# Converting the last stage's weights further ahead of the blocks that use them (three chained layers, one Trainium2 core)

## The chip, the cores and the metric

The program runs on one core of one Trainium2 chip. The metric is the device time of one execution in microseconds (us). The kernel before takes 586.35 us (median of three runs, 586.0 to 589.92).

## The reference

Three layers stand one behind the other; the first two are told in short, since the change touches only the third.

```python
def _moe2_ref(x, w_in, w_out):            # x: 1536 x 512, d_ff = 2048
    h = x @ w_in
    r = np.maximum(h, 0.0)
    g = r * r
    return (g @ w_out).astype(np.float32)

def reference(**kwargs):
    attn_out = _attn_ref(**attn_kwargs)   # windowed attention with block summaries
    x = attn_out.transpose(0, 2, 1, 3).reshape(B * S, H * D)
    x = _moe_ref(x=x, **moe_kwargs)       # each token to one of 8 experts, 192 tokens each
    return _moe2_ref(x=x, **moe2_kwargs)
```

All data are float32.

## The kernel before, in words

`attention` computes the first layer, `moe` the second and the third. The last stage of `moe` is the third layer. Its input x stands in the on-chip tiles `yhi` and `ylo`: a value rounded to the narrower type fp32r, and what the rounding leaves. The weights `w_in` and `w_out` are split in the same way into `whi` and `wlo`, and each product is made of three matmuls (hi x hi, lo x hi, hi x lo).

**Blocks.** The stage has 48 blocks: 3 groups `j` of 512 tokens, and in each 16 slices `f` of 128 columns of d_ff (L1071). `hmm(i)` (L1074) makes one 128 x 512 slice of h with 12 matmuls (L1083) into a PSUM tile `pg`, of which there are four. ScalarE (ACT) takes the relu (L1086) into `xa` or `xb`, VectorE (DVE) squares it (L1087), ACT rounds it (L1092) and DVE takes the rest (L1093); both go to a tile `xt` or `ht`. `omm(i)` (L1096) multiplies that with `w_out`: 12 matmuls (L1110) into the accumulators `ph` and `px`. The loop at L1130 gives TensorE (PE) first `hmm(i)`, then `omm(i - 2)` (`LAG = 2`), so a block's own second half follows two blocks later.

**Conversion.** The weights come in as 32 pieces of 128 x 512 values, each a pair of 32-bit words per value (L613: four quarters of d_ff, in each four pieces of `w_in`, then four of `w_out`). `conv_stream` (L635) makes a piece usable in four steps, and each step puts one instruction on DVE: L647, L651 and L657 assemble the float32 value `f` from the raw words, then ACT rounds it into the hi tile (L650) and DVE subtracts for the lo tile (L654). The rounding of a piece stands in the second step of the piece behind it and its subtraction in the third, so piece n is done with the third step of piece n + 1; `ndone` (L655) counts the finished pieces, `nstep` the steps. The raw words lie in a tile `raw` with two buffers; when L657 has read a piece, SyncE's queue issues the load of the piece two further on (L662, L627). A piece lands in the hi and lo tiles of its quarter, named `w2a`, `w2b` or `w`.

**When steps are placed.** Some steps are recorded while the experts of the second layer run (L1019): 60 steps are recorded ahead of block 0, so 14 pieces are done there. In the last stage there are three sources: one step inside each block, behind the square (L1088); `SF` steps behind each block (L1139, `SF` at L417); and a `while` loop ahead of a block (L1134), which puts as many steps as are missing until `need` pieces are done. `need` (L1133) is what block i itself uses: for `hmm(i)` all four `w_in` pieces of quarter i // 4, for `omm(i - 2)` the `w_out` pieces up to its own. There are 4 steps to a block, so the steps recorded ahead of block i are 60 + 4i until the `while` loop has to help; it has to at block 12, whose quarter ends with piece 27.

The order of the instructions on each engine is that in which the program records them (`manual_schedule`, L1155): DVE takes squares, rests and conversion steps in one row, and an instruction that waits holds those behind it.

Of the kernel before, what the change touches and what calls it, by code (L numbers as in the profile page):

```python
# [413 lines left out]

BIG = 2.0 ** 120
CS = 2.0 ** 100
SF = 3  # L417


class Clock:  # L420
# [175 lines left out]
def moe(tc, nc, R0, x_dram, m_dram, L9, w1, w2, win, wout, out, identf, identb, dbg=None):  # L596
# [74 lines left out]
    def conv_step(n=1):  # L671
        for _ in range(n):
            if w2b or nstep[0] < 32:
                nstep[0] += 1
                next(CST, None)
# [396 lines left out]
    LAG = 2  # L1072

    def hmm(i):  # L1074
        j, f = seq[i]
        ps = p_g.tile([128, 512], F32, name="pg")
        whi, wlo = W[0, f // 4]
        fs = slice(128 * (f % 4), 128 * (f % 4) + 128)
        js = slice(512 * j, 512 * j + 512)
        n = 0  # L1080
        for k in range(4):
            for a, b in ((whi, yhi), (wlo, yhi), (whi, ylo)):
                nc.tensor.matmul(ps, a[:, k, fs], b[:, k, js], start=(n == 0), stop=(n == 11))  # L1083
                n += 1
        r = f1.tile([128, 512], F32, name="xa" if i % 2 else "xb")
        nc.scalar.activation(r, ps, AF.Relu)  # L1086
        nc.vector.tensor_tensor(r, r, r, op=OP.mult)  # L1087
        conv_step()  # L1088
        nm = ("xt", "xt", "ht")[i % 3]
        gg = f1.tile([128, 2, 512], F32R, name=nm, bufs=2 if nm == "xt" else 1)  # L1090
        ghi, glo = gg[:, 0, :], gg[:, 1, :]
        nc.scalar.activation(ghi, r, AF.Copy)  # L1092
        nc.vector.tensor_tensor(glo, r, ghi.bitcast(F32), op=OP.subtract)  # L1093
        GG[i] = ghi, glo
# [34 lines left out]

    for i in range(len(seq) + LAG):  # L1130
        if i < len(seq):
            last = i - LAG
            need = max(8 * (i // 4) + 4 if i < 16 else 0, 8 * (last // 4) + 5 + last % 4 if 0 <= last else 0)  # L1133
            while ndone[0] < min(len(todo), need):  # L1134
                conv_step()
            hmm(i)
        if i >= LAG:
            omm(i - LAG)
        conv_step(SF)  # L1139
    ctx.close()  # L1140


@with_exitstack
def kernel(ctx: ExitStack, tc: tile.TileContext, q, k, v, wg, w1, w2, win, wout, out):
    nc = tc.nc
    const = ctx.enter_context(tc.tile_pool(name="const", bufs=1))
    dram = ctx.enter_context(tc.tile_pool(name="dram", bufs=1, space=bass.MemoryType.DRAM))
    identf = const.tile([128, 128], F32, name="identf")
    make_identity(nc, identf)
    identb = const.tile([128, 128], BF, name="identb")  # L1150
    nc.vector.tensor_copy(identb, identf)
    L9 = const.tile([128, NBLK, E + 1], F32, name="L9")
    x_dram = dram.tile([N, DM], F32, name="x_dram")
    m_dram = [dram.tile([N], F32, name=f"m_dram{i}") for i in range(E)]
    ctx.enter_context(tc.manual_schedule())  # L1155
    route = Route(tc, nc, L9, identf)
    with ExitStack() as actx:
        attention(actx, tc, nc, q, k, v, wg, x_dram, L9, identf, identb, route)
    moe(tc, nc, route, x_dram, m_dram, L9, w1, w2, win, wout, out, identf, identb)
# [29 lines left out]
```

## Time and profile before

| | |
|---|---|
| median of the runs (three) | 586.35 us (586.0 to 589.92) |
| the profiled execution's own time | 587.83 us |
| span of its instructions | 585.6 us |
| TensorE (PE) matmul busy | 569.4 us, 97% of the span |
| VectorE (DVE) busy | 342.8 us, 59% |
| ScalarE (ACT) busy | 197.4 us, 34% |
| granted TensorE clock, mean | 0.996 of full speed |

The span runs from the first to the last instruction that the profiler recorded; the rest of the execution's time lies around it. Busy times are sums of the instructions of an engine. Matmuls overlap one another, so PE's distance from start to start is what counts, not the length of one row. A releaser behind an arrow is the instruction that ended a wait.

### The profile page before, as it was taken

What the parts mean: (1) busy time and instruction counts of PE and PEld (TensorE: products, weight loads), DVE (VectorE), ACT (ScalarE), POOL (GpSimd) and SP (SyncE); (2) the same over time, 40 slices, a digit from 0 to 9 for tenths busy, and PEclk for the clock granted to TensorE, in tenths of its full rate; (3) what the DMA queues carried; (4) which work ended last, traced back from release to release, by engine and by line L of the source; (5) the groups of instructions that cost most, each with busy time, mean ns of one, the idle gap of its engine ahead of it and who ended that gap; (6) DMA issues with size and microseconds to landing.
All of it is one profiled execution on the core that took longest, in us unless ns stands there. A gap on an engine that the chain in (4) does not pass through costs nothing.

```text
span 585.6 us, 10523 instructions
## 1 busy us (share of the span) xinstructions
PE 569.4 (97%) x4131; PEld 475.4 (81%) x4131; DVE 342.8 (59%) x773; ACT 197.4 (34%) x421; POOL 79.7 (14%) x136
## 2 busy tenths in 40 slices
PE   7999998999999999999999999799999999999996
PEld 4778873698998989899998888588888888888884
DVE  5885688877878779766566766663322222222222
ACT  4887861331422314123223333232222122222221
POOL 6564400210201132020000000000300000300002
PEclk9999999999999999999999999999999999999999
DMA  8997224645644455789742323320100000100001
GB/s 223 240 200 144 92 75 140 225 136 203 226 160 160 156 199 179 253 265 403 234 157 72 113 105 108 109 72 2 72 2 0 1 0 1 72 1 0 1 0 72
DMA packets 55392, 71.33 MB, mean 122 GB/s; under 512 B 21296, under 2 KB 32560, under 8 KB 55344
## 3 DMA queue, kind: packets, MB, share of 16 engines
q1 hardware_dynamic: 53360, 64.38, 35.5%
q0 software_dynamic: 1984, 6.29, 3.1%
q8 instruction: 32, 0.52, 0.4%
q14 instruction: 16, 0.13, 0.1%
HBM read 64.37 MB, written 6.29 MB: 121 GB/s over the span
## 4 chain that ended last, share of the span: by engine, by line
PE 76%; issue 13%; DVE 4%; DMA 2%; POOL 1%; ACT 1%; SPq 1%; POOLq 0%; DVEq 0%; ACTq 0%
PE pg L1083 15%; PE ph L976 15%; PE ph L993 15%; PE ph L1110 11%; PE px L1110 4%; PE O L284 2%; PE cnt L582 2%; DMA rawq<-in_q_dram 2%; PE T L270 2%; DVE G L570 2%; PE S L250 2%; POOL out_dram L1123 1%; PE ms L534 1%; PE T L193 1%; PE T L321 1%
## 5 line engine op out<-in xcount | busy, mean ns | idle before, releaser
L976 PE MATMUL ph<-xt,w 128*128 128x192 f32 x512 | 90.6, 330 | 0.0
L570 DVE TENSOR_SCALAR G<-mrow,m 128x1536 bf16<-128x1536 f32 (+4 forms) x108 | 84.7, 839 | 8.1 <-ACT mrow L537 4.8
L993 PE MATMUL ph<-ht,w 128*128 128x192 f32 x512 | 89.4, 329 | 0.0
L993 PEld LDWEIGHTS ph<-ht,w 128*128 128x128 f32 x512 | 82.9, 190 | 2.9 <-issue 2.5
L976 PEld LDWEIGHTS ph<-xt,w 128*128 128x128 f32 x512 | 82.5, 190 | 2.8 <-issue 2.1
L1083 PE MATMUL pg<-yhi,w 128*128 128x512 f32 x192 | 60.0, 392 | 3.2 <-DVE w L654 2.2
L1087 DVE TENSOR_TENSOR xa<-xa 128x512 f32<-128x512 f32 x24 | 16.6, 693 | 65.9 <-ACT xa L1086 65.9
L1087 DVE TENSOR_TENSOR xb<-xb 128x512 f32<-128x512 f32 x24 | 16.6, 693 | 62.9 <-ACT xb L1086 62.9
L1123 POOL DMA_INDIRECT out_dram<-f,sci x6 | 5.9, 978 | 306.7 <-DVE f L1121 306.1
L1083 PEld LDWEIGHTS pg<-yhi,w 128*128 128x128 f32 x192 | 36.0, 188 | 12.3 <-DVE w L654 3.1
L1086 ACT ACTIVATE xa<-pg 128x512 f32<-128x512 f32 x24 | 14.4, 599 | 78.2 <-PE pg L1083 78.2
L1086 ACT ACTIVATE xb<-pg 128x512 f32<-128x512 f32 x24 | 14.4, 599 | 73.7 <-PE pg L1083 73.7
L981 ACT ACTIVATE ht<-ph 128x384 f32<-128x384 f32 x32 | 15.7, 491 | 65.2 <-PE ph L976 61.5
L1083 PE MATMUL pg<-ylo,w 128*128 128x512 f32 x96 | 37.4, 389 | 0.0
L1110 PE MATMUL ph<-w,xt 128*128 128x512 f32 x144 | 36.8, 402 | 0.0
L1110 PEld LDWEIGHTS ph<-w,xt 128*128 128x128 f32 x144 | 28.0, 194 | 6.0
L1083 PE MATMUL pg<-yhi,w2a 128*128 128x512 f32 x96 | 29.7, 391 | 0.0
L1083 PE MATMUL pg<-yhi,w2b 128*128 128x512 f32 x96 | 29.6, 389 | 0.0
L999 ACT ACTIVATE yhi<-ph 128x384 fp32r<-128x384 f32 x16 | 7.9, 492 | 58.4 <-PE ph L993 58.4
L263 ACT ACTIVATE P<-S,nm 128x120 f32<-128x120 f32 x96 | 26.7, 374 | 2.4 <-DVE nm L259 2.4
L905 POOL DMA_INDIRECT xa<-x_dram,sci x8 | 10.8, 1355 | 87.2 <-DVE sci L893 65.3
L1083 PEld LDWEIGHTS pg<-yhi,w2b 128*128 128x128 f32 x96 | 18.0, 188 | 3.8
(245 smaller groups left out, 984.4 us busy)
## 6 DMA issues: line engine op xcount, KB each, us to landing
w<-in_moe_w_dram SPq DMA_DIRECT2D x64, 512.0 KB, 6.1
raw<-in_moe_w_in_dram SPq DMA_DIRECT2D x14, 512.0 KB, 4.0
raw<-in_moe_w_out_dram SPq DMA_DIRECT2D x14, 512.0 KB, 3.2
vw<-in_v_dram SPq DMA_DIRECT2D x16, 240.0 KB, 6.7
rawk<-in_k_dram SPq DMA_DIRECT2D x8, 384.0 KB, 6.8
rawq<-in_q_dram SPq DMA_DIRECT2D x8, 384.0 KB, 6.6
x_dram<-x SPq DMA_DIRECT2D x10, 256.0 KB, 2.3
w<-in_moe_w_in_dram SPq DMA_DIRECT2D x2, 512.0 KB
```

Of the source, the lines that this page charges most:

```text
L250: nc.tensor.matmul(ss[hh][64 * par:64 * par + 64, i, :], QT[b, hp][r, 128 * c + 64 * par:128 * c + 64 * par + 64], KW_[b, hp][r, 2 * c + p ...
L263: nc.scalar.activation(P[u][:, hh, i], SS[u][hh][:, i], AF.Exp, bias=NM[u][:, hh, i:i + 1])
L270: nc.tensor.transpose(ps[0:KW, i, :], P[u][:, hh, i, :], identf)
L570: self.nc.vector.tensor_scalar(t[:, used:used + w], self.mrow[:, 128 * j0:128 * j1], self.m[:, c:c + 1], CS, op0=OP.is_le, op1=OP.mult)
L976: nc.tensor.matmul(ps[:, j, 0:CAP], w[:, k, 128 * (f % 4):128 * (f % 4) + 128], d["xt"][:, k, :], start=(k == 0), stop=(k == 3), skip_grou ...
L981: nc.scalar.activation(d["ht"][:, f0:f0 + 2, :], ps[:, :, 0:CAP], AF.Relu)
L993: nc.tensor.matmul(ps[:, j, 0:CAP], w[:, f % 4, 128 * dd:128 * dd + 128], d["ht"][:, f, :], start=(f == 0), stop=(f == 7), skip_group_chec ...
L1083: nc.tensor.matmul(ps, a[:, k, fs], b[:, k, js], start=(n == 0), stop=(n == 11))
L1086: nc.scalar.activation(r, ps, AF.Relu)
L1087: nc.vector.tensor_tensor(r, r, r, op=OP.mult)
L1110: nc.tensor.matmul(PO[j][t], a[:, 128 * t:128 * t + 128], b[:, f % 4, :], start=(f == 0 and n == 0), stop=(f == 15 and n == 2))
L1123: sc = nc.gpsimd.indirect_dma_start(out=out, out_offset=bass.IndirectOffsetOnAxis(ap=sci[:, 4 * j + t:4 * j + t + 1], axis=0), in_=o, in_o ...
```

## The change

Two edits in the last stage. `SF` becomes 4: five conversion steps to a block, one inside and four behind. And the `while` loop ahead of block i asks for what block i + 2 uses: the `w_in` quarter of `hmm(i + 2)` and the `w_out` piece of `omm(i)`.

```diff
-SF = 3
+SF = 4
...
     for i in range(len(seq) + LAG):
         if i < len(seq):
-            last = i - LAG
-            need = max(8 * (i // 4) + 4 if i < 16 else 0, 8 * (last // 4) + 5 + last % 4 if 0 <= last else 0)
+            need = max(8 * ((i + LAG) // 4) + 4 if i + LAG < 16 else 0, 8 * (i // 4) + 5 + i % 4)
             while ndone[0] < min(len(todo), need):
                 conv_step()
             hmm(i)
```

The number of instructions on each engine stays as it was; PE's row and SyncE's row keep their order, DVE's and ACT's rows are interleaved in another way.

First place: DVE before, from block 9's square (`xa`, first row) to block 10's (`xb`) and on to its rest. `w_4648` is the lo tile of `w_out`'s third quarter, `w_4806` that of `w_in`'s fourth.

```order
L1087 TENSOR_TENSOR xa<-xa 128x512
L651 SCALAR_TENSOR_TENSOR f<-raw,f 128x512
L1093 TENSOR_TENSOR xt<-xa,xt 128x512
L654 TENSOR_TENSOR w_4648<-f,w_4647 128x512
L657 SCALAR_TENSOR_TENSOR f<-raw,f 128x512
L647 TENSOR_SCALAR f<-raw 128x512
L1087 TENSOR_TENSOR xb<-xb 128x512
L651 SCALAR_TENSOR_TENSOR f<-raw,f 128x512
L1093 TENSOR_TENSOR xt<-xb,xt 128x512
```

Each block has its square, one step, its rest and three steps; piece 24, the first of the fourth quarter, is not yet finished here.

The same place on DVE now, from block 9's square to block 10's. `w_4760` is the lo tile of `w_in`'s fourth quarter.

```order
L1087 TENSOR_TENSOR xa<-xa 128x512
L654 TENSOR_TENSOR w_4760<-f,w_4759 128x512
L1093 TENSOR_TENSOR xt<-xa,xt 128x512
L657 SCALAR_TENSOR_TENSOR f<-raw,f 128x512
L647 TENSOR_SCALAR f<-raw 128x512
L651 SCALAR_TENSOR_TENSOR f<-raw,f 128x512
L654 TENSOR_TENSOR w_4760<-f,w_4759 128x512
L657 SCALAR_TENSOR_TENSOR f<-raw,f 128x512
L647 TENSOR_SCALAR f<-raw 128x512
L651 SCALAR_TENSOR_TENSOR f<-raw,f 128x512
L654 TENSOR_TENSOR w_4760<-f,w_4759 128x512
L1087 TENSOR_TENSOR xb<-xb 128x512
```

Block 9 has one step and four, and the `while` loop ahead of block 10 adds the four rows from the second L657 on; the last L654 finishes piece 27.

Second place: DVE before, from block 11's rest (`ht`) to block 12's square (`xb`), with `w_4806` as above.

```order
L1093 TENSOR_TENSOR ht<-xa,ht 128x512
L654 TENSOR_TENSOR w_4806<-f,w_4805 128x512
L657 SCALAR_TENSOR_TENSOR f<-raw,f 128x512
L647 TENSOR_SCALAR f<-raw 128x512
L651 SCALAR_TENSOR_TENSOR f<-raw,f 128x512
L654 TENSOR_TENSOR w_4806<-f,w_4805 128x512
L657 SCALAR_TENSOR_TENSOR f<-raw,f 128x512
L647 TENSOR_SCALAR f<-raw 128x512
L651 SCALAR_TENSOR_TENSOR f<-raw,f 128x512
L654 TENSOR_TENSOR w_4806<-f,w_4805 128x512
L1087 TENSOR_TENSOR xb<-xb 128x512
```

Three steps are block 11's own and six are the `while` loop's; the last L654 finishes piece 27, which block 12's own first half reads.

The same place now: block 11's rest to block 12's square. `w_4871` is the lo tile of `w_out`'s fourth quarter.

```order
L1093 TENSOR_TENSOR ht<-xa,ht 128x512
L651 SCALAR_TENSOR_TENSOR f<-raw,f 128x512
L654 TENSOR_TENSOR w_4871<-f,w_4870 128x512
L657 SCALAR_TENSOR_TENSOR f<-raw,f 128x512
L647 TENSOR_SCALAR f<-raw 128x512
L1087 TENSOR_TENSOR xb<-xb 128x512
```

Only block 11's own four steps stand here, and they belong to `w_out`.

## Rows read from the trace of the kernel before

**Rows 1.** The page: the span, and PE's busy tenths in 40 equal slices.

```profile
span 585.6 us, 10523 instructions
...
PE   7999998999999999999999999799999999999996
```

**Rows 2.** The chain that ended last around 370: start us, us, what.

```profile
366.78 2.73 PE pg L1083 x12
373.55 3.21 DMA raw<-in_moe_w_out_dram
379.39 3.64 PE ph L1110 x9
```

**Rows 3.** Waits from 301 to 586: total us, times, longest us.

```profile
PEld pg L1083 <- DVE w L654: 3.1, 3, 2.0
PE pg L1083 <- DVE w L654: 2.2, 2, 1.7
...
PE pg L1083 <- ACT w L650: 1.1, 2, 0.5
```

**Rows 4.** Timeline of PE, blocks 11 to 13: start us, us, instruction, [idle before].

```profile
366.62 0.61 PE L1083 MATMUL pg<-yhi,w 128*128 128x512 f32 x2
...
369.34 2.20 PE L1110 MATMUL ph<-w,xt 128*128 128x512 f32 x9
...
372.06 0.61 PE L1083 MATMUL pg<-yhi,w 128*128 128x512 f32 x2
...
378.66 0.50 PE L1083 MATMUL pg<-yhi,w 128*128 128x512 f32 x1 [1.66 <-DVE w L654]
...
379.23 3.80 PE L1110 MATMUL ph<-w,xt 128*128 128x512 f32 x9
...
383.56 0.61 PE L1083 MATMUL pg<-yhi,w 128*128 128x512 f32 x2
```

**Rows 5.** Windows: stretch, length, busy us of PE, PEld, DVE, ACT, POOL; clock, DMA.

```profile
312.00:372.06 60.06, 60.06 (x268) 49.72 (x266) 41.02 (x70) 21.81 (x37) 0.00 (x0) 1.00 0.32 104
...
377.50:383.56 6.06, 4.90 (x15) 3.88 (x15) 4.41 (x8) 1.83 (x3) 0.00 (x0) 0.72 0.29 107
...
383.56:495.00 111.44, 111.44 (x493) 92.33 (x492) 34.90 (x53) 27.52 (x45) 4.82 (x8) 1.00 0.04 16
```

**Rows 6.** Timeline of DVE in block 12, out of the `while` loop's steps.

```profile
372.83 0.69 DVE L657 SCALAR_TENSOR_TENSOR f<-raw,f 128x512 int32<-128x512 int32 x1
...
376.85 0.43 DVE L647 TENSOR_SCALAR f<-raw 128x512 int32<-128x512 int32 x1 [1.06 <-DMA raw<-in_moe_w_out_dram]
...
377.92 0.68 DVE L654 TENSOR_TENSOR w<-f,w 128x512 fp32r<-128x512 f32 x1
```

**Rows 7.** Timeline of DVE, block 9 from its square to block 10's square.

```profile
359.35 0.69 DVE L1087 TENSOR_TENSOR xa<-xa 128x512 f32<-128x512 f32 x1 [1.81 <-ACT xa L1086]
359.96 0.68 DVE L651 SCALAR_TENSOR_TENSOR f<-raw,f 128x512 int32<-128x512 int32 x1
...
361.35 0.69 DVE L654 TENSOR_TENSOR w<-f,w 128x512 fp32r<-128x512 f32 x1
361.95 0.69 DVE L657 SCALAR_TENSOR_TENSOR f<-raw,f 128x512 int32<-128x512 int32 x1
362.56 0.42 DVE L647 TENSOR_SCALAR f<-raw 128x512 int32<-128x512 int32 x1
...
364.79 0.69 DVE L1087 TENSOR_TENSOR xb<-xb 128x512 f32<-128x512 f32 x1 [1.81 <-ACT xb L1086]
```

**Rows 8.** The source line L627 from 310 to 400: its loads, issue to landing.

```profile
DMA to landing us min/median/max: 3.1/3.7/4.5
```

**Rows 9.** Timeline of DVE and PE at the stage's start, blocks 0 and 1.

```profile
317.16 0.69 DVE L1093 TENSOR_TENSOR xt<-xb,xt 128x512 fp32r<-128x512 f32 x1
...
318.37 0.69 DVE L657 SCALAR_TENSOR_TENSOR f<-raw,f 128x512 int32<-128x512 int32 x1
...
320.38 2.20 PE L1110 MATMUL ph<-w2a,xt 128*128 128x512 f32 x9
...
323.17 0.43 DVE L647 TENSOR_SCALAR f<-raw 128x512 int32<-128x512 int32 x1 [0.58 <-DMA raw<-in_moe_w_in_dram]
```

## The prediction

> **What bounds the kernel now.** I read the page first. PE's row is made of nines but for the first, seventh and last slice and a 7 in the 26th of 40, which runs from 366.0 to 380.6 us (585.6 / 40 = 14.64 each) [rows 1]. The chain that ended last comes next: around that place it consists of PE's matmuls, leaves PE for a load of raw weights at 373.55, and is back on PE at 379.39 [rows 2]. Then the waits of the last stage: PE and its weight loads wait there for nothing but the converted weights, released by L654 on DVE and L650 on ACT [rows 3]. PE's timeline gives the price [rows 4]. A block is 5.44 us from start to start (366.62 to 372.06): 2.72 for the first half (L1083), 2.72 for the second (L1110). Block 12, which starts at 372.06, takes until 383.56, which is 11.50. So one block is 6.06 late. No other stretch of the stage holds such a loss: PE is busy for all of the 60.06 us ahead of it and all of the 111.44 behind it, at a clock of 1.00 [rows 5].
>
> The 6.06 has two parts. The first half of block 12 lasts 7.17 (372.06 to 379.23) where 2.72 is normal: 4.45 of waiting. The second half lasts 4.33 (379.23 to 383.56) where 2.72 is normal, though nothing is waited for: 1.61 that the lower clock costs. The granted clock from 377.50 to 383.56 is 0.72 on the mean, a mixture of the two levels 1.2 and 2.4 GHz, after an engine that had been stopped four times [rows 4, 5].
>
> Why it waits: 60 + 4 x 12 = 108 steps stand ahead of block 12, and piece 27 is done with step 4 x 28 + 2 = 114. The six missing steps are placed between block 11 and block 12, and PE reads the pieces as they come. One of the six also waits 1.06 for its raw words, because the load could be issued only after L657 at 372.83 [rows 6].
>
> **The change part by part.** Nothing is added or removed on any engine; the 68 steps left for the stage (128 less 60) come sooner.
>
> *SF from 3 to 4.* Steps ahead of block i become 60 + 5i. That is 110 ahead of block 10 and 115 ahead of block 11, so step 114 falls among block 10's own: this edit alone would finish piece 27 before block 12. Its cost lies on DVE. In a block of before, DVE works from the square at 359.35 to the end of the third late step at 362.98, 3.63 us, and is then idle for 1.81 until the next square at 364.79 [rows 7]. Steps follow one another by 0.57 on the mean (0.61, 0.60 and 0.61 for the three long ones, 0.46 for L647). A fifth step makes it 4.20 of 5.44 and leaves 1.24 idle. On the path this is 0: PE hides it, as long as DVE's waits stay under 1.24 per block.
>
> What DVE may wait for is the raw words. A load is issued when L657 of the piece two earlier is through, and L647 needs it five steps later. With five steps to a block that is one block from start to start, 5.44, or 4.75 from the end of L657. From the end of one L657 (318.37 + 0.69 = 319.06) to the L647 that waited for its load (323.17) it took 4.11 [rows 9]; landing alone takes 3.1 to 4.5 [rows 8]. I take 4.11, the row that holds issue and landing together: 0.64 is left, so no wait in regular blocks. With 4.5 and the same 0.1 of issue it would still fit, by 0.15.
>
> The stage's start is the tight place, since the first three first-halves follow each other by 2.72. Block 0's rest (L1093) ends at 317.85 and is needed by the second half at 320.38 [rows 9]: 2.53 to spare, and the added step stands behind it. For block k the need moves by 5.44 and DVE's row by 4.20 plus waits, so the room is 2.53 + 1.24k minus the waits so far. One wait of 0.58 is in the rows [rows 9]; with the fifth step I expect some 0.5 to 1 for each of the first four blocks, less than the room gained. Cost 0.
>
> *The look-ahead.* Ahead of every block up to 9 the 60 + 5i steps already satisfy it. At block 10 it asks for 28 pieces, step 114, with 110 done: four steps are placed ahead of block 10's square. PE's times up to there are those of before, so block 9's rows serve [rows 7]. L657 of piece 26 stands where L654 was, 361.35 to 362.04, and frees the buffer for piece 28. Three steps follow, then the burst: L657 at 363.6, and L647 of piece 28, ready at 364.2. Its load lands 4.11 after 362.04, at 366.15 (by the longest landing 366.65), a new wait of 1.9 to 2.4. Behind it in DVE's row stand two steps and block 10's square. Piece 27 is done 1.76 after the wait, at 367.9 to 368.4. PE reads it from 372.06 on: 3.7 to 4.2 to spare. The square of block 10 starts at 367.3 to 367.8, up to 3.0 later than the 364.79 of before, and the rest ends by 369.9; PE needs it at 374.78 (372.06 + 2.72). 4.9 to spare. What else hangs on the square is a PSUM tile that PE wants four blocks on. So the burst is hidden, and cost and gain of the look-ahead by itself are 0; without the fifth step it would have had to place 14 steps there (114 - 100), about 8 us and more loads to wait for.
>
> *What is late next.* The `w_out` pieces: second half 12 needs piece 28 and comes behind block 14's first half; 120 steps stand ahead of block 12 and step 118 is enough. All 32 pieces are done in block 12 or 13, about three blocks sooner. Nothing is late.
>
> **The sum.** Against the profiled execution: 587.83 - 6.06 = 581.77; the 2.23 around its span stays. The runs have a median of 586.35, 1.48 lower. The wait of 4.45 follows from the order of instructions and the length of the steps, so it is in every run. Of the 1.61 I can't say that: the profiled execution is longer than the median by nearly this much, so the runs may have had less of it. From the median the ends are 586.35 - 4.45 = 581.90 and 586.35 - 6.06 = 580.29. I take half of the clock's share, 4.45 + 0.81 = 5.26, as nothing in the rows puts it nearer to one end: 581.1.
>
> **Rivals.**
> *The whole clock share is in every run.* The clock falls because the engine stands still, so what removes the standstill gives back 1.61 too: 580.3. For it: 0.72 here, and 1.00 ahead and behind [rows 5]. Against it: the distance of the profiled execution from the median. By the Trainium skill, page "TensorE: Matmul & The Clock Gate", section "Part 1: The HAM clock gate", the slow clock is the state of an idle engine and steady work releases it; by that rule the time is this rival's, and the trace agrees in the one execution that it shows. The same section says that the point of the change moves from run to run, which speaks for less than the whole in some.
>
> *A part of the wait stays.* If loads under the quicker pace take so long that piece 27 is later than 372.06, block 12 waits again. That needs some 4 us more than I worked out, and the DMA engines are busy for 0.32 of their time there [rows 5]. If half of the stall stays, 583.3.
>
> *DVE becomes the bound, and it is slower.* The place is DVE's row in blocks 0 to 12. If each block waits for raw words by w, the lag grows by w - 1.24 a block. Over 13 blocks, less the room of 2.53 at the start, PE would lose 13(w - 1.24) - 2.53; this passes 6.06 from w = 1.90 on. With w = 2.3, about the burst's wait in every block, it loses 11.3 and the time is 586.35 - 5.26 + 11.3 = 592.4. Against it: in the blocks of before DVE waits for the square and not for loads [rows 7], and 4.75 is more than the longest landing [rows 8].
>
> *The change doesn't do what it says.* Excluded by the order: the last L654 of the awaited tile stands ahead of block 10's square.
>
> **How the numbers follow.** Forecast (581.1, its own range 580.3 to 581.9) 0.54; whole clock share (580.3) 0.33; a part stays (583.3) 0.10; slower 0.03. A run can tell about 1% here, which is 5.86 us, time 580.49. Three quarters of the whole-share case and a third of the forecast's lie beyond it, 0.25 + 0.18 = 0.43. Slower by over 1% has only its own case, 0.03; the rest, 0.54, is within 1%. The range takes the two ends of the sum, 1.1 below for the scatter of the runs (their lowest is 0.35 under the median), and above the case in which half of the stall stays: 579.2 to 584.0.
>
> **What would show it.** Right: in the profile after, all blocks from 3 on are 5.44 apart, PE's waits for L654 and L650 in the last stage are gone, the slice with the 7 is a 9, the clock is 1.00 there, and the conversions end about three blocks sooner. DVE shows a wait of about 2 at an L647 ahead of block 10's square, and PE none behind it. Wrong: a wait of PE for `xt` or `ht` (L1093) in blocks 0 to 12, for W pieces at block 12, or a stretch below clock 1.00 without a wait.

## The result, and the profile after

The changed kernel takes 581.17 us (median of four runs, 580.91 to 581.62); the kernel before, with one more run, 586.6 (586.0 to 589.92). The ratio is 0.9897, with a 95% interval of 0.9859 to 0.9934: 5.4 us less, and the interval reaches from 3.9 to 8.3. The forecast was 581.1. The profiled execution took 581.22.

The page of the changed kernel, its span and PE's busy tenths, which answer to [rows 1]:

```profile
span 579.0 us, 10522 instructions
...
PE   6999998999999999999999999999999999999995
```

The 7 in the 26th slice has become a 9. The span is 6.6 shorter than before. TensorE's timeline shows where that is; it answers to [rows 4] and holds the starts of blocks 11, 12 and 13:

```profile
366.06 0.62 PE L1083 MATMUL pg<-yhi,w 128*128 128x512 f32 x2
...
371.50 0.62 PE L1083 MATMUL pg<-yhi,w 128*128 128x512 f32 x2
...
374.21 2.20 PE L1110 MATMUL ph<-w,xt 128*128 128x512 f32 x9
...
376.94 0.62 PE L1083 MATMUL pg<-yhi,w 128*128 128x512 f32 x2
```

Block 12 takes 5.44 (371.50 to 376.94) like its neighbours, where it took 11.50. That is 6.06. The other 0.56 lies ahead of the stage: block 0 starts at 311.47 where it started at 312.03, though nothing was changed ahead of it, and block 11 at 366.06 where it started at 366.62. Such shifts from execution to execution are why the blocks are compared here and not the spans. The windows answer to [rows 5]; the columns are the same:

```profile
312.00:372.06 60.06, 60.06 (x266) 49.68 (x266) 49.26 (x84) 23.45 (x40) 0.00 (x0) 1.00 0.40 128
372.06:383.56 11.50, 11.50 (x53) 9.51 (x52) 8.26 (x14) 4.26 (x8) 0.00 (x0) 1.00 0.11 42
383.56:495.00 111.44, 111.44 (x493) 92.30 (x492) 30.30 (x45) 27.35 (x45) 7.08 (x13) 1.00 0.03 12
```

PE is busy throughout and the clock is 1.00. DVE's work has moved forward: 49.26 ahead of 372.06 where it was 41.02, and less behind. In the waits from 295 on, the rows of PE for L654 and L650 [rows 3] are gone. What is left is 0.3 of PE's weight loads for L1093, which the kernel before had too, and DVE's waits for raw words:

```profile
DVE f L647 <- DMA raw<-in_moe_w_out_dram: 2.4, 4, 1.2
...
PEld ph L1110 <- DVE ht L1093: 0.3, 1, 0.3
```

Two of these four waits, 1.0 in all, lie ahead of the stage. In the stage DVE waits 1.4 for raw words, where it waited 1.8 before. (`w_in` and `w_out` come as 64-bit values: on the page, the load of one 128 x 512 piece is 512 KB. So not all data are float32, and this is why the pieces have to be converted.)

The burst that the look-ahead places ahead of block 10's square, in DVE's timeline, out of its rows:

```profile
360.78 0.68 DVE L657 SCALAR_TENSOR_TENSOR f<-raw,f 128x512 int32<-128x512 int32 x1
...
363.05 0.69 DVE L657 SCALAR_TENSOR_TENSOR f<-raw,f 128x512 int32<-128x512 int32 x1
364.90 0.43 DVE L647 TENSOR_SCALAR f<-raw 128x512 int32<-128x512 int32 x1 [1.16 <-DMA raw<-in_moe_w_out_dram]
365.36 0.69 DVE L651 SCALAR_TENSOR_TENSOR f<-raw,f 128x512 int32<-128x512 int32 x1
365.97 0.68 DVE L654 TENSOR_TENSOR w<-f,w 128x512 fp32r<-128x512 f32 x1
366.57 0.69 DVE L1087 TENSOR_TENSOR xb<-xb 128x512 f32<-128x512 f32 x1
```

The reader is to see a real wait of 1.16 that costs nothing: L654 finishes piece 27 at 366.65, and block 12 starts at 371.50. The last conversion ends at 379.79, in block 13; in the kernel before it ended at 400.74, in block 16.

### The profile page after: what moved, and what is told of

It is laid out like the page before. It is cut to its first block, busy times and chain, and to the rows that moved or that the text cites. A ratio compares the mean times of both kernels' runs of the same rounds, so it can differ in the third digit from the quotient of the medians.

```text
span 579.0 us, 10522 instructions
## 1 busy us (share of the span) xinstructions
PE 565.8 (98%) x4131; PEld 473.7 (82%) x4131; DVE 343.7 (59%) x773; ACT 197.0 (34%) x421; POOL 78.6 (14%) x136
## 3 DMA queue, kind: packets, MB, share of 16 engines
q0 software_dynamic: 1984, 6.29, 3.2%
HBM read 64.37 MB, written 6.29 MB: 122 GB/s over the span
## 4 chain that ended last, share of the span: by engine, by line
PE 78%; issue 14%; DVE 3%; DMA 2%; POOL 1%; SPq 1%; ACT 1%; POOLq 0%; DVEq 0%; ACTq 0%
PE pg L1083 16%; PE ph L976 15%; PE ph L993 15%; PE ph L1110 11%; PE px L1110 4%; PE O L284 2%; PE cnt L582 2%; PE T L270 2%; DMA rawq<-in_q_dram 2%; DVE G L570 2%; PE S L250 2%; POOL out_dram L1123 1%; PE ms L534 1%; PE T L193 1%; PE T L321 1%
## 5 line engine op out<-in xcount | busy, mean ns | idle before, releaser
L1083 PE MATMUL pg<-yhi,w 128*128 128x512 f32 x192 | 59.1, 389 | 0.0
L1087 DVE TENSOR_TENSOR xa<-xa 128x512 f32<-128x512 f32 x24 | 16.6, 691 | 60.1 <-ACT xa L1086 60.0
L1087 DVE TENSOR_TENSOR xb<-xb 128x512 f32<-128x512 f32 x24 | 16.6, 691 | 59.6 <-ACT xb L1086 59.6
L1083 PEld LDWEIGHTS pg<-yhi,w 128*128 128x128 f32 x192 | 36.0, 188 | 7.5
L1083 PE MATMUL pg<-ylo,w 128*128 128x512 f32 x96 | 37.3, 389 | 0.0
L1086 ACT ACTIVATE xb<-pg 128x512 f32<-128x512 f32 x24 | 14.3, 596 | 65.7 <-PE pg L1083 65.7
L1086 ACT ACTIVATE xa<-pg 128x512 f32<-128x512 f32 x24 | 14.3, 596 | 63.5 <-PE pg L1083 63.5
L1110 PE MATMUL ph<-w,xt 128*128 128x512 f32 x144 | 35.2, 389 | 0.0
L1110 PEld LDWEIGHTS ph<-w,xt 128*128 128x128 f32 x144 | 27.0, 188 | 5.6
L1083 PE MATMUL pg<-yhi,w2a 128*128 128x512 f32 x96 | 29.7, 391 | 0.0
L1083 PE MATMUL pg<-yhi,w2b 128*128 128x512 f32 x96 | 29.6, 389 | 0.0
L1083 PEld LDWEIGHTS pg<-yhi,w2b 128*128 128x128 f32 x96 | 18.0, 188 | 3.8
```

What stands on the lines that cost most here:

```text
L1110: nc.tensor.matmul(PO[j][t], a[:, 128 * t:128 * t + 128], b[:, f % 4, :], start=(f == 0 and n == 0), stop=(f == 15 and n == 2))
```

## The experiments

Seven series of runs stand beside runs of the kernel before, with intervals, and the kernel before was profiled twice more. Runs of the first four share a chip (the kernel before there: 587.68, 11 runs), and so do the next three (587.41, 11 runs).

**Only the fifth step.**

```diff
-SF = 3
+SF = 4
```

> Only SF = 4, the look-ahead as before. Theory A (the fifth step alone finishes piece 27 in time; step 114 falls among block 10's own): the same time as the changed kernel, 5.3 to 5.6 us under the kernel before, no wait of TensorE for L654 or L650 in the last stage, and no burst ahead of block 10's square, so no wait of VectorE for raw words there. Rival (the look-ahead is what removes the wait): block 12 still waits, time near 586.

Measured: 580.88 us, ratio 0.9886 (0.9867 to 0.9905). TensorE has no wait for a weight piece. DVE's timeline around block 10:

```profile
361.75 0.68 DVE L654 TENSOR_TENSOR w<-f,w 128x512 fp32r<-128x512 f32 x1
363.52 0.69 DVE L1087 TENSOR_TENSOR xb<-xb 128x512 f32<-128x512 f32 x1 [1.09 <-ACT xb L1086]
...
366.59 0.69 DVE L654 TENSOR_TENSOR w<-f,w 128x512 fp32r<-128x512 f32 x1
367.19 0.68 DVE L657 SCALAR_TENSOR_TENSOR f<-raw,f 128x512 int32<-128x512 int32 x1
368.96 0.69 DVE L1087 TENSOR_TENSOR xa<-xa 128x512 f32<-128x512 f32 x1 [1.08 <-ACT xa L1086]
```

There is no burst: DVE is idle for 1.09 ahead of a block's square, and piece 27 is finished at 367.28, ahead of block 12 at 370.79. The fifth step alone does it; the rival is out. The gain is 6.8 (5.6 to 7.8 by the interval), more than the 5.3 to 5.6 that was expected.

**Only the look-ahead.** The new `need` line of the change, with `SF = 3`.

> Only the look-ahead, SF stays 3. Theory A (steps follow each other by 0.57 us and each load lands some 4 us after the L657 that frees its buffer): 14 steps stand ahead of block 10's square, 8 us of work and two or three load waits of 1 to 2 us, so piece 27 is done at about 374.2, as block 12 begins to need it, and block 10's rest (L1093) ends at 375.5 to 376.3 where TensorE wants it at 374.8: a new wait of 0.7 to 1.5 us at the second half of block 10, released by L1093 in place of L654; time 4 to 5 us under the kernel before. Rival (the look-ahead alone hides everything, as it asks two blocks early): no wait, 5.3 to 5.6 us under the kernel before.

Measured: 583.1 us, ratio 0.9935 (0.9910 to 0.9960), 4.6 below the kernel before and 2.2 above the kernel with only the fifth step. The 14 steps and their three load waits, in DVE's timeline, and behind them block 10's square and rest:

```profile
365.64 0.43 DVE L647 TENSOR_SCALAR f<-raw 128x512 int32<-128x512 int32 x1 [1.46 <-DMA raw<-in_moe_w_in_dram]
...
368.66 0.43 DVE L647 TENSOR_SCALAR f<-raw 128x512 int32<-128x512 int32 x1 [0.65 <-DMA raw<-in_moe_w_in_dram]
...
371.68 0.43 DVE L647 TENSOR_SCALAR f<-raw 128x512 int32<-128x512 int32 x1 [0.67 <-DMA raw<-in_moe_w_out_dram]
...
373.36 0.69 DVE L1087 TENSOR_TENSOR xb<-xb 128x512 f32<-128x512 f32 x1
...
374.74 0.69 DVE L1093 TENSOR_TENSOR xt<-xb,xt 128x512 fp32r<-128x512 f32 x1
```

TensorE's timeline of the same kernel, blocks 12 and 13:

```profile
371.34 0.62 PE L1083 MATMUL pg<-yhi,w 128*128 128x512 f32 x2
...
374.76 0.50 PE L1110 MATMUL ph<-w,xt 128*128 128x512 f32 x1 [0.52 <-ACT xt L1092]
375.49 2.11 PE L1110 MATMUL ph<-w,xt 128*128 128x512 f32 x8 [0.23 <-DVE xt L1093]
...
378.11 0.61 PE L1083 MATMUL pg<-yhi,w 128*128 128x512 f32 x2
```

The weights arrive in time, if only just (piece 27 is finished at 373.43, and the three matmuls of block 12 that read it start at 373.38, with its hi tile), and the wait has moved: TensorE now wants block 10's rounded square (L1092), then its rest (L1093), which stood in DVE's row behind the burst. Blocks 12 to 13 are 6.77 apart in place of 5.44, 1.33 lost. The wait is the size that was expected, except that ACT's L1092 releases its first part. The runs lose 2.2 against the fifth step, more than the 1.33 of this trace. Two of the four runs took 582.39 and 582.45 at a mean granted clock of 0.998, the others 583.74 and 585.35 at 0.994 and 0.995. So the clock may have fallen behind this wait too in some runs, but no trace of such a run is kept: this is not shown.

**TensorE kept busy in the waits of block 12.** The kernel before, and 15 matmuls whose result nobody reads:

```diff
+        fill = {6: 2, 7: 3, 9: 2, 10: 8} if i == 12 else {}
+        spare = p_g.tile([128, 4, 128], F32, name="pg") if fill else None
         for k in range(4):
             for a, b in ((whi, yhi), (wlo, yhi), (whi, ylo)):
+                for _ in range(fill.get(n, 0)):
+                    nc.tensor.matmul(spare, identb, identb[:, None, :].to_broadcast([128, 4, 128]), start=True, stop=True)
```

> The kernel before, with 15 dummy matmuls (128x512 of identb into a spare pg tile) in block 12's four waits: 2, 3, 2 and 8 of them, about 3.3 us where TensorE now stands still for about 4.1. Nothing else moves, so the 4.45 us of waiting stays. Theory A (the clock falls because TensorE stands still): the clock stays at 1.00 there, the second half of block 12 takes 2.72 in place of 4.33, and the profiled span is about 1.6 under that of before; the timed runs get shorter by as much as they had of the clock's share: 1.6 if every run has it, about 0.8 if half. Rival (the clock's fall has another cause, or the runs without a profile don't have it): the time stays within 0.3 us of before.

Measured: 585.3 us, ratio 0.9956 (0.9940 to 0.9972), which is 1.6 to 3.5 us less than before, though nothing got shorter but the time that matmuls take. TensorE's timeline of block 12 (L1087 is L1083 of before, L1114 is L1110, and L1086 the added matmuls):

```profile
374.55 0.62 PE L1087 MATMUL pg<-yhi,w 128*128 128x512 f32 x2
...
379.34 1.90 PE L1086 MATMUL pg<-identb 128*128 128x512 bf16 x8
381.21 0.50 PE L1087 MATMUL pg<-yhi,w 128*128 128x512 f32 x1
...
381.78 2.23 PE L1114 MATMUL ph<-w,xt 128*128 128x512 f32 x9
...
384.53 0.62 PE L1087 MATMUL pg<-yhi,w 128*128 128x512 f32 x2
```

The first half takes 7.23 (374.55 to 381.78), as long as the 7.17 of [rows 4]: the wait is all there. The second half takes 2.75 where it took 4.33. The two halves in windows, of this kernel:

```profile
374.55:381.78 7.23, 7.06 (x28) 3.17 (x27) 5.42 (x10) 1.26 (x2) 0.00 (x0) 1.00 0.43 146
381.78:384.53 2.75, 2.75 (x13) 2.25 (x12) 1.76 (x3) 1.73 (x3) 0.00 (x0) 1.00 0.00 0
```

And of the kernel before:

```profile
372.06:379.23 7.17, 3.95 (x13) 2.02 (x12) 5.41 (x10) 1.26 (x2) 0.00 (x0) 1.00 0.44 147
379.23:383.56 4.33, 4.33 (x14) 3.39 (x12) 3.31 (x6) 1.83 (x3) 0.00 (x0) 0.61 0.24 81
```

So the clock falls because TensorE stands still, and the fall has a price of its own behind the wait. The mean granted clock that is listed for each run agrees: 0.990 to 0.996 in the 22 runs of the kernel before that stand beside the experiments, 0.997 to 0.999 in six of the seven runs of this one. The seventh is the profiled one, at 0.993. Its span is no help, contrary to what was expected of it: its stage started later (block 12 at 374.55, not 372.06), after a granted clock of 0.91 in its first 20 us and 0.96 from 80 to 120, where the first profile of before has 1.00.

**Eight steps to a block.** The changed kernel with `SF = 7`.

> The changed kernel with SF = 7, eight steps to a block. VectorE then has 8 x 0.57 + 1.4 = 6.0 us of work for each block of 5.44, and two loads per block, of which each piece pair takes 4.1 + 2.3 = 6.4 at least. Theory A (VectorE's row becomes the bound once its work and waits pass 5.44 a block): the lag grows by 0.6 to 1.2 a block over the 8 blocks in which steps are left, 5 to 10 us, and the room at the start is 2.5, so TensorE waits 2 to 7 us for L1093 in blocks 1 to 9, and the time is 2 to 7 us above the changed kernel. Rival (TensorE's four pg tiles and the two-block lag hide that too): the same time as the changed kernel.

Measured: 593.58 us, ratio 1.0092 (1.0069 to 1.0115): slower than the kernel before, and 12.7 above the kernel with only the fifth step. The mechanism is the expected one, the size is not. DVE's timeline, two squares and the load waits ahead of them:

```profile
338.27 0.43 DVE L647 TENSOR_SCALAR f<-raw 128x512 int32<-128x512 int32 x1 [1.09 <-DMA raw<-in_moe_w_out_dram]
338.62 0.69 DVE L1087 TENSOR_TENSOR xa<-xa 128x512 f32<-128x512 f32 x1
...
345.15 0.43 DVE L647 TENSOR_SCALAR f<-raw 128x512 int32<-128x512 int32 x1 [0.99 <-DMA raw<-in_moe_w_out_dram]
345.49 0.69 DVE L1087 TENSOR_TENSOR xb<-xb 128x512 f32<-128x512 f32 x1
```

The squares are 6.87 apart, 1.43 over a block's 5.44. TensorE's blocks 3 and 12 start at 324.16 and 385.28: 61.12 for nine blocks that take 48.96, so 12.2 are lost, in blocks 4 to 10. Most of it is waits of TensorE for L1092 and then L1093, but not all, as the second halves in blocks 6 and 7 show:

```profile
346.89 0.49 PE L1110 MATMUL ph<-w2b,xt 128*128 128x512 f32 x1 [0.60 <-ACT xt L1092]
347.62 2.11 PE L1110 MATMUL ph<-w2b,xt 128*128 128x512 f32 x8 [0.23 <-DVE xt L1093]
...
354.70 0.51 PE L1110 MATMUL ph<-w2b,ht 128*128 128x512 f32 x1 [1.58 <-ACT ht L1092]
355.43 3.67 PE L1110 MATMUL ph<-w2b,ht 128*128 128x512 f32 x8 [0.22 <-DVE ht L1093]
```

Behind the longer wait of block 7 the same eight matmuls take 3.67 in place of 2.11, at a granted clock of 0.65 from 354.70 to 359.63. Block 7 takes 9.39, the six others 6.29 to 7.08 each. So about 1.6 of the 12.2 is the clock's share, which the expectation did not have at all; and it took 0.6 to 1.2 of lag a block, where the squares above show 1.43.

**The change again, the fifth step again, and six steps to a block,** beside each other. The third is the changed kernel with `SF = 5`.

> The changed kernel once more, beside the next two on one chip. Theory A (all 6.06 of block 12 goes, the clock's share too): 5.4 to 6.7 us under the kernel before. Rival (only the waiting of 4.45 goes in runs without a profile): 4.4 to 4.8 under it.

> SF = 4 alone, beside the changed kernel on one chip. Theory A (the look-ahead costs and brings nothing beside the fifth step): within 0.5 us of the changed kernel. Rival (the burst ahead of block 10 costs something that the trace doesn't show on TensorE): 0.5 to 1.5 us faster than it.

> The changed kernel with SF = 5, six steps to a block: 6 x 0.57 + 1.35 = 4.8 of 5.44 on VectorE, and a load of raw words for every 3.6 us. Theory A (VectorE's row is covered until its work and its waits pass 5.44 a block; with two loads in flight a piece can't be had faster than every 3.3 us or so): VectorE waits up to 1 us in some blocks, the lag stays under the room of 2.5, TensorE doesn't wait, the same time as the changed kernel within 0.5 us. Rival (the room is used up here already): TensorE waits for L1092 or L1093 in blocks 1 to 8, 1 to 3 us above the changed kernel.

Measured: the change 580.88, ratio 0.9883 (0.9862 to 0.9904); the fifth step alone 581.32, ratio 0.9903 (0.9877 to 0.9929); six steps 581.24, ratio 0.9892 (0.9872 to 0.9911). The three are one time within their intervals. The change gains 6.5 here (587.41 to 580.88), 5.6 to 8.1 by the interval: that holds the whole 6.06 and leaves out the 4.45 of the waiting alone. In the traces of all three, blocks 3 to 47 are 5.44 apart, so no cost or gain of the look-ahead shows beside the fifth step. With six steps DVE waits for loads, at most 0.8 at once, and TensorE still doesn't wait: the room lasts to six steps and is gone with eight.

**The kernel before, profiled twice more.**

> The kernel before, for a second profile: does the clock fall in block 12 in other executions too, and for how long? Theory A (it falls because TensorE stands still there, in every execution): the first half of block 12 takes about 7.2 again, and the second half more than 2.72, by 0.8 to 2.5, with a granted clock under 1.00. Rival (the fall was particular to the first profile): the second half takes 2.72.

> The same kernel a third time, with the same expectations as the second profile.

Measured: 587.2 and 588.28 us. TensorE's timeline, blocks 12 and 13, of the first:

```profile
371.44 0.62 PE L1083 MATMUL pg<-yhi,w 128*128 128x512 f32 x2
...
378.79 3.61 PE L1110 MATMUL ph<-w,xt 128*128 128x512 f32 x9
...
382.93 0.62 PE L1083 MATMUL pg<-yhi,w 128*128 128x512 f32 x2
```

And of the second:

```profile
371.85 0.62 PE L1083 MATMUL pg<-yhi,w 128*128 128x512 f32 x2
...
379.49 3.99 PE L1110 MATMUL ph<-w,xt 128*128 128x512 f32 x9
...
384.01 0.62 PE L1083 MATMUL pg<-yhi,w 128*128 128x512 f32 x2
```

Block 12 takes 11.49 and 12.16, so 6.05 and 6.72 are lost. The granted clock of the second halves is 0.64 and 0.58. It is low already at the end of the first half, which takes 7.35 and 7.64 in place of 7.17. In all three executions that were profiled, then, the clock falls, and its share is 1.6 to 2.3 (6.05 and 6.72 less 4.45).

## Why the prediction was right, point by point

- *One block is late, by 6.06.* Right: block 12 is back at 5.44, and no other block changed.
- *SF from 3 to 4 costs nothing and finishes piece 27 in time.* Right, and shown by the kernel that has this edit alone. DVE's idle time in a regular block is 1.09 in it; worked out was 1.24.
- *The loads keep up with five steps.* Right where it matters, and a little short in the term: landing took up to 5.0 in the changed kernel, not 4.5, and VectorE waits for loads ahead of block 10's square (1.2) and in block 11 (0.3). That lies in the room. The waits of 0.5 to 1 that were expected in each of the first four blocks did not come: DVE's timeline has no wait for a load from block 0's square (315.20) to that of block 10's burst.
- *The burst ahead of block 10 is hidden.* Right. Its wait is 1.16, worked out was 1.9 to 2.4. The term was mis-sized because 4.11, a round trip of a `w_in` piece, was taken for a `w_out` piece: from the end of one L657 (361.46) to the L647 that waited (364.90) it was 3.44. [rows 6] had a row for this very piece: 3.33, from 373.52 to 376.85. Piece 27 had 4.85 to spare, where 3.7 to 4.2 was worked out.
- *The look-ahead alone would need 14 steps ahead of block 10.* Right as an order, and its price was left open: it is 1.33 in the trace of the second experiment.
- *"I take half of the clock's share".* This step was wrong: the term 0.81 should have been the whole 1.61 or more. The share is whole in each of three profiled executions (1.6 to 2.3), and the timed runs have it too: taking only the clock's fall away brought 1.6 to 3.5, and the later gains, 6.8 (5.6 to 7.8) for the fifth step alone and 6.5 (5.6 to 8.1) for the change, leave out the 5.26 of the sum. The reason given, that the profiled execution is 1.48 above the median and may hold a share that the runs don't, doesn't hold; executions differ by as much ahead of the last stage (block 0 starts between 310.7 and 314.5 in the profiles). So the rival with the whole share was the true case: 6.06 to 6.7 for block 12. That the forecast's 581.1 came within 0.1 of the measured 581.17 is luck: the four runs then at hand gave 5.4, and their interval (3.9 to 8.3) can't tell 5.26 from 6.06.
- *Faster by over 1%: 0.43.* With the whole share this should have been the larger part; the two measurements of the change say 1.0% and 1.2%.
- *The slower rival, DVE as the bound.* Its place and releaser are as described, shown with eight steps to a block, though ACT's L1092 releases the larger part of each wait. Its threshold, a wait of 1.9 a block, was worked out for five steps, which leave VectorE idle; no run tests it. With eight steps the work alone is 6.0 by estimate, over a block's 5.44, and waits of about 1 come on top, as the squares 6.87 apart show.

By the Trainium skill, page "TensorE: Matmul & The Clock Gate", section "Part 1: The HAM clock gate", activity releases the throttle and the default is the slow clock. The trace agrees: the same wait with matmuls in it keeps 1.00, and without them the second half runs at 0.61.

## What to carry to other kernels

A stall of the engine that sets the end is worth more than its idle time when the clock falls with it: read how long the work behind it takes too, and compare blocks, not spans. Preparation that is asked for just when it is used comes as a burst in another engine's row; spread it one step more per block, and it fits into idle time that is already there. Work out the room from both sides: here one step more of 0.57 in 1.81 of idle time removed the stall, a burst alone moved it to what stood behind the burst, and four steps more put blocks 4 to 10 at the pace of VectorE's row.

## What the runs showed that had not been expected

The clock fell although TensorE did not stand still in one piece: in block 12's wait of 4.45 (3.22 of it idle in PE's rows) it ran a matmul now and then, with no idle stretch longer than 1.66 by the profile [rows 4], and 15 short matmuls in these gaps were enough to hold 1.00. With eight steps to a block it fell too, behind the longest of the waits (1.58, in block 7). In a stage that a wait can't be taken out of, such filling alone is worth 0.4% here (0.28 to 0.60).
